# Attention probabilities turned by the DMA engines instead of TensorE, in a fused attention and gated feed-forward kernel

## The chip, the cores and the metric

The kernel runs on one core of a Trainium2 chip. Its metric is the device time of one execution in microseconds (us). The core has a matrix engine (TensorE, PE in the profile; its weight loads are listed apart as PEld), three engines for element-wise work (VectorE = DVE, ScalarE = ACT, GpSimd = POOL), a queue that here issues all transfers (SyncE = SP), and 16 DMA engines that carry them. Each engine works off its own list of instructions in order; an instruction that waits for a semaphore holds back everything behind it on its engine.

## The reference

The kernel computes attention with 4 batches, 8 heads, 768 positions and a head size of 64, and a gated feed-forward layer behind it, all in float32:

```python
scores = scale * np.matmul(q, k.transpose(0, 1, 3, 2))
keep = is_global | is_local            # 8 global columns, 96 local ones
scores = np.where(keep, scores + bias, -1e9)
a = np.exp(scores - np.max(scores, axis=-1, keepdims=True))
a = a / (np.sum(a, axis=-1, keepdims=True) + 1e-09)
attn = np.matmul(a, v)                 # then laid out as x: 3072 x 512
gate = 1.0 / (1.0 + np.exp(-(x @ w_gate)))
val = x @ w_val
return (gate * val @ w_out)            # d_ff = 1536
```

## The kernel before

The 3072 tokens are cut into 8 **blocks** of 384 tokens (index `bi`, `NB` = 384), two to a batch. A block's attention is done in 12 **items** `(s, t)`: `s` is one of 4 pairs of heads, `t` one of 3 tiles of 128 tokens. A block's feed-forward part is done in 12 **units** `f`, one for each slice of 128 of `d_ff`. Float32 products are made of three products of split operands (a high part and a low one, `xh`/`xl`, `w1h`/`w1l`, `w2h`/`w2l`, `hh`/`hl`).

A unit is `ff_in` (L527: twelve matmuls into the PSUM bank `ps_g`, twelve into `ps_u`, with a tanh on ScalarE at L545, a product on VectorE at L554, the split into `hh` on ScalarE at L557 and into `hl` on VectorE) and, later, `ff_out` (L561: nine matmuls into `ps_o`). The weights of `ff_out` are split again for each unit (L217 on ScalarE, then GpSimd). The weight conversion that the first part of the program needs is over when the third block's attention starts.

An item runs through these steps:

- `scores` (L359): matmuls into `ps_s`, then on VectorE two fused "add a table, take the minimum" instructions (L406), then on ScalarE two exponentials with their sums (L419). The query positions of a block's tile see a window of 256 key columns, 128 for the first tile of a batch.
- `normalise` (L425): on VectorE the sum's reciprocal (L434, L436) and two products (L438) in the tile `sb`, named `work` in the profile.
- `transposes` (L440): on TensorE four transposes of 128x128 (two for a batch's first tile) into the PSUM bank `ps_t` (L449), then one copy of that bank to `pT` in SBUF, on ScalarE (L457) for all blocks that this text is about.
- `values` (L460), after three items of each of two pairs of heads: matmuls with `pT` (L476) for the third block on into `ps_t` and `ps_v`, then `xh` on ScalarE (L518) and `xl` on VectorE (L519). The result is the `x` of the next block's feed-forward units.

From the third block on (`bi > PAIR`, `PAIR` = 1) a block's 12 items go beside the 12 units of the block before it, one item to a unit. `split_step` (L331) prepares `ks` and `qs` for a pair of heads on ScalarE, VectorE and GpSimd; `load_step` (L289) loads a pair's inputs through SP.

The order of the code sets priorities only: a scheduler at build time lays the instructions of each engine into a fixed order, and each engine keeps to it. Tiles that are named with `bufs` share so many buffers, and a writer waits until the last reader of its buffer is done. SP issues all loads and stores in one fixed order too.

Of the kernel before, what the change touches and what calls it, by code (L numbers as in the profile page):

```python
# [8 lines left out]
F32 = mybir.dt.float32  # L9
# [3 lines left out]
I16 = mybir.dt.int16  # L13
# [6 lines left out]
P = 128  # L20
# [8 lines left out]
def attn_moe_kernel(ctx, tc, qT, kT, v, n_global, n_local, wg, wv, wo, out, B, H, S, D):  # L29
    nc = tc.nc  # L30
# [5 lines left out]
    TB = 3  # L36
    NB = TB * P
    WORKB = 4
    OSTB = 4
    PTB = 3  # L40
    QB = 2
    SCALE = 1.0 / float(D) ** 0.5
# [13 lines left out]
    spool = inner.enter_context(tc.tile_pool(name="spool", bufs=2))  # L56
# [3 lines left out]
    late = {}  # L60
# [13 lines left out]
    words = cpool.tile([P, 2, 2], I32, name="words")  # L74
# [193 lines left out]
    PAIR = 1  # L268
    blocks = [(b, t0, TB) for b in range(B) for t0 in range(0, NTB, TB)]
# [14 lines left out]
    steps = {}  # L284
# [66 lines left out]
    def bank(*names):  # L351

        i = turns.get(names, 0)
        turns[names] = i + 1
        name = names[i % len(names)]
        pool = {"ps_s": ps_a, "ps_t": ps_a, "ps_v": ps_a, "ps_g": ps_gv, "ps_u": ps_gv}.get(name, ps_o)
        return pool.tile([P, 4 * P], F32, name=name)
# [82 lines left out]
    def transposes(bi, s, t):  # L440
        st = steps[bi, s]
        b, t0, nt = blocks[bi]
        n = 1 if t0 + t == 0 else 2
        sb, _ = st.pop(("s", t))
        pt = bank("ps_t", "ps_o0") if bi < PAIR else bank("ps_t")
        pt = pt.rearrange("p (c x) -> p c x", c=4)
        for j in range(2):
            for c in range(n):
                nc.tensor.transpose(pt[:, n * j + c], sb[:, j, c * P:(c + 1) * P], ident)  # L449
        if bi > PAIR and s % 2:  # L450
            pT = late["pool"].tile([P, 4, P], F32, name="pT2", bufs=PTB)
        else:
            pT = spool.tile([P, 4, P], F32, name="pT", tag="pT", bufs=PTB)
        if bi < PAIR and t > 0:
            nc.vector.tensor_copy(pT[:, 0:2 * n], pt[:, 0:2 * n])
        else:
            nc.scalar.copy(pT[:, 0:2 * n], pt[:, 0:2 * n])  # L457
        st["pT"][t] = pT

    def values(bi, pairs):  # L460
# [100 lines left out]
    def ff_out(bi, f):  # L561
# [26 lines left out]
        if f == NF - 1:  # L588
            for t in range(nt):
                ot = late["pool"].tile([P, DM], F32, name="ost", bufs=OSTB)  # L590
                if t == nt - 1 and end:
# [46 lines left out]
    def run(kind, bi, s, t):  # L638
        if kind == "S":
            if t == 0 and (bi, s) == (0, 0):  # L640
                ready_step((bi, s))
            scores(bi, s, t)
            if t == blocks[bi][2] - 1:
                i = all_steps.index((bi, s))
                if i + 1 < len(all_steps) and all_steps[i + 1] != (PAIR + 1, 0):
                    ready_step(all_steps[i + 1])
        elif kind == "T":
            normalise(bi, s, t)
            transposes(bi, s, t)
        else:  # L650
            if bi <= PAIR:
                values(bi, (s,))
            elif s % 2:
                values(bi, (s - 1, s))
# [153 lines left out]
    with tc.If(redo > 0):  # L808
        with tc.For_i(0, B, 1) as b:
            for t0 in range(0, NTB, TB):  # L810
                blocks.append((b, t0, TB))
                bi = len(blocks) - 1
# [45 lines left out]
```

## Time and profile before

| | |
|---|---|
| time, median of 3 runs | 772.47 us (769.70 to 772.59) |
| the profiled execution | 771.78 us, its span 770.0 us |
| TensorE clock granted, mean | 0.99 |
| TensorE busy | 755.6 us, 98% of the span |
| TensorE weight loads | 682.3 us, 89% |
| VectorE | 405.6 us, 53% |
| ScalarE | 408.8 us, 53% |
| GpSimd | 213.2 us, 28% |
| DMA moved | 57.01 MB, 74 GB/s over the span |

The span is the time from the first to the last instruction; some 2 us lie around it. A matmul's end is modelled, so what a group of matmuls costs is read from the distance of the starts, not from the busy time. Names such as `pT` or `work` are those of tiles; in `out<-in` the written tile stands first. A row of a timeline gives start and length in us; a row of a source line gives the shortest, the middle and the longest duration in ns.

### The profile page before, as it was taken

The numbers are of one execution on the slowest core, as the hardware profiler recorded it, in microseconds if no ns is written. First come the engines' busy times: TensorE is split into PE (matmuls) and PEld (weight loads), VectorE is DVE, ScalarE is ACT, GpSimd is POOL, SyncE is SP. The second block draws the span as 40 slices with busy tenths as digits, with TensorE's granted clock in tenths as the row PEclk, the third lists the DMA queues.
The fourth block names the chain that finished last, engine by engine and source line by source line (L and its number), as shares of the span: only waits on it lengthen the run. The fifth ranks groups of instructions, "written<-read, shape, count | busy, mean of one in ns | idle before, by whom it ended". The sixth has DMA issues, their size and how long they took to land. (4 is left out here: it accounts for less than half of the span.)

```text
span 770.0 us, 12641 instructions
## 1 busy us (share of the span) xinstructions
PE 755.6 (98%) x4661; PEld 682.3 (89%) x4661; DVE 405.6 (53%) x1085; ACT 408.8 (53%) x944; POOL 213.2 (28%) x164
## 2 busy tenths in 40 slices
PE   8999999999999999999999999999999999999996
PEld 5767678899999999999999999999999999999995
DVE  6789887556445555554565544454654565221111
ACT  4689876645546555553556554464555555432222
POOL 5424234332313323221232322222221222112222
PEclk7999999999999999999999999999999999999998
DMA  8768553403022121122113110221211200000001
GB/s 255 218 214 263 179 194 91 120 14 92 8 73 77 34 75 33 39 83 58 37 37 92 60 54 20 68 74 37 71 37 42 78 25 17 1 10 33 1 0 46
DMA packets 66982, 57.01 MB, mean 74 GB/s; under 512 B 17248, under 2 KB 59232, under 8 KB 66912
## 3 DMA queue, kind: packets, MB, share of 16 engines
q1 hardware_dynamic: 66912, 56.12, 24.7%
q8 instruction: 39, 0.64, 0.3%
q14 instruction: 31, 0.25, 0.1%
HBM read 49.81 MB, written 6.29 MB: 73 GB/s over the span
## 5 line engine op out<-in xcount | busy, mean ns | idle before, releaser
L180 POOL TENSOR_TENSOR w2l<-w2f,w2h 128x512 fp32r<-128x512 f32 x87 | 114.0, 1310 | 414.3 <-ACT w2h L217 406.3
L554 DVE SCALAR_TENSOR_TENSOR work<-work,ps_u 128x384 f32<-128x384 f32 x88 | 48.7, 553 | 216.7 <-PE ps_u L537 207.8
L537 PE MATMUL ps_u<-xh,w1l 128*128 128x384 f32 x384 | 134.4, 350 | 0.0
L537 PE MATMUL ps_g<-xh,w1l 128*128 128x384 f32 x384 | 131.3, 342 | 1.2 <-ACT work L545 1.2
L537 PE MATMUL ps_g<-xl,w1h 128*128 128x384 f32 x384 | 130.4, 339 | 0.7 <-DVE xl L519 0.7
L537 PE MATMUL ps_u<-xl,w1h 128*128 128x384 f32 x384 | 129.9, 338 | 0.0
L537 PE MATMUL ps_g<-xh,w1h 128*128 128x384 f32 x384 | 129.9, 338 | 0.0
L537 PE MATMUL ps_u<-xh,w1h 128*128 128x384 f32 x384 | 129.9, 338 | 0.0
L557 ACT ACTIVATE hh<-work 128x384 fp32r<-128x384 f32 x88 | 46.0, 522 | 128.0 <-DVE work L554 128.0
L419 ACT ACTIVATE work<-work,nms 128x256 f32<-128x256 f32 (+1 forms) x192 | 92.0, 481 | 27.4 <-DVE nms L406 27.0
L577 PE MATMUL ps_o<-w2l,hh 128*128 128x512 f32 x261 | 104.7, 401 | 0.7 <-POOL w2l L180 0.6
L577 PE MATMUL ps_o<-w2h,hh 128*128 128x512 f32 x261 | 102.7, 394 | 0.0
L577 PE MATMUL ps_o<-w2h,hl 128*128 128x512 f32 x261 | 102.6, 394 | 0.0
L217 ACT ACTIVATE w2h<-w2f 128x512 fp32r<-128x512 f32 x87 | 54.9, 631 | 89.6 <-PE ps_o L577 88.6
L180 DVE TENSOR_TENSOR hl<-work,hh 128x384 fp32r<-128x384 f32 x88 | 69.3, 788 | 28.9 <-ACT hh L557 28.7
L537 PEld LDWEIGHTS ps_g<-xh,w1l 128*128 128x128 f32 x384 | 72.3, 188 | 5.2 <-issue 2.6
L537 PEld LDWEIGHTS ps_g<-xl,w1h 128*128 128x128 f32 x384 | 72.2, 188 | 3.0 <-DVE xl L519 1.1
L537 PEld LDWEIGHTS ps_u<-xh,w1l 128*128 128x128 f32 x384 | 72.3, 188 | 1.1 <-issue 0.2
L537 PEld LDWEIGHTS ps_u<-xl,w1h 128*128 128x128 f32 x384 | 72.4, 189 | 0.5
L537 PEld LDWEIGHTS ps_g<-xh,w1h 128*128 128x128 f32 x384 | 72.2, 188 | 0.7
L537 PEld LDWEIGHTS ps_u<-xh,w1h 128*128 128x128 f32 x384 | 72.2, 188 | 0.2 <-issue 0.2
L406 DVE CUSTOM_DVE_ANT_0 work<-ps_s,tab 128x256 f32<-128x256 f32 x136 | 52.7, 420 | 25.4 <-PE ps_s L387 25.0
(131 smaller groups left out, 1169.1 us busy)
## 6 DMA issues: line engine op xcount, KB each, us to landing
qr<-in_qT SPq DMA_DIRECT2D x56, 192.0 KB, 3.3
kr<-in_kT SPq DMA_DIRECT2D x32, 192.0 KB, 2.6
v<-in_v SPq DMA_DIRECT2D x32, 192.0 KB, 3.1
raw<-in_w_gate SPq DMA_DIRECT2D x12, 512.0 KB, 4.2
raw<-in_w_val SPq DMA_DIRECT2D x12, 512.0 KB, 5.8
raw<-in_w_out SPq DMA_DIRECT2D x12, 512.0 KB, 3.8
out<-ost SPq DMA_DIRECT2D x24, 256.0 KB, 2.2
v<-in_v SPq DMA_DIRECT2D x16, 144.0 KB, 2.7
```

Source lines behind the costliest of these rows:

```text
L180: eng.tensor_tensor(out, a, b, op=ALU.subtract)
L217: ins = nc.scalar.activation(hi, w, AF.Copy)
L406: ins = nc.vector.tensor_tensor_reduce(sb[:, j, :w], ps[j][:, :w], (tabs0 if zero else tabs)[2 * s + j], -SCALE, 3.0e38, op0=ALU.add, op1= ...
L419: ins = nc.scalar.activation(sb[:, j, :w], sb[:, j, :w], AF.Exp, scale=-1.0, bias=nm[:, j:j + 1], accum_out=sm[:, j:j + 1])
L537: nc.tensor.matmul(ps[:, :n], wt[f][:, i, c], xt[:, c, :n], start=(k == 0), stop=(k == 3 * NC - 1))
L554: nc.vector.scalar_tensor_tensor(a[:, :n], a[:, :n], 1.0, pss[1][:, :n], op0=ALU.add, op1=ALU.mult)
L557: nc.scalar.activation(hh[:, :n], a[:, :n], AF.Copy)
L577: ins = nc.tensor.matmul(outs[bi][t], ht[:, t * P:(t + 1) * P], wt, start=(f == 0 and k == 0), stop=(f == NF - 1 and k == len(parts) - 1),)
```

## The change

For the blocks from the third on, `transposes` no longer uses TensorE. VectorE takes the 32-bit probabilities apart into two planes of 16-bit halves (two copies into `halves`, one for the low and one for the high halves of all columns); one DMA transpose on SP turns both planes from `halves` to `turned`; ScalarE copies the turned low halves and VectorE the turned high halves into the interleaved places of `pT`. `values` is unchanged. `halves` has one buffer, `turned` two, and the output tile `ost` has three buffers where it had four.

```diff
-    OSTB = 4
+    OSTB = 3
...
     def transposes(bi, s, t):
         sb, _ = st.pop(("s", t))
+        if bi > PAIR:
+            st["pT"][t] = transposes_by_dma(s, n, sb)
+            join(bi, s, t)
+            return
         pt = bank("ps_t", "ps_o0") if bi < PAIR else bank("ps_t")
...
+    def transposes_by_dma(s, n, sb):
+        m = 2 * n
+        halves = late["pool"].tile([P, 2 * 4 * P], I16, name="halves")[:, 0:2 * m * P]
+        words = sb[:, :, 0:n * P].bitcast(I16).rearrange("p j (x h) -> p j x h", h=2)
+        for h in range(2):
+            dst = halves[:, h * m * P:(h + 1) * m * P].rearrange("p (j x) -> p j x", j=2)
+            nc.vector.tensor_copy(dst, words[:, :, :, h])
+        turned = late["pool"].tile([P, 2 * 4, P], I16, name="turned", bufs=2)[:, 0:2 * m]
+        nc.sync.dma_start_transpose(turned, halves)
+        return turned
+
+    def join(bi, s, t):
+        turned = st["pT"][t]
+        m = 2 if blocks[bi][1] + t == 0 else 4
+        if s % 2:
+            pT = late["pool"].tile([P, 4, P], F32, name="pT2", bufs=PTB)
+        else:
+            pT = spool.tile([P, 4, P], F32, name="pT", tag="pT", bufs=PTB)
+        words = pT[:, 0:m].bitcast(I16).rearrange("p c (x h) -> p c x h", h=2)
+        nc.scalar.copy(words[:, :, :, 0], turned[:, 0:m])
+        nc.vector.tensor_copy(words[:, :, :, 1], turned[:, m:2 * m])
```

How the change moves instructions is shown at two places. The first is VectorE in the sixth block's attention, between two items of its second pair of heads. Before, the normalising products (L438) of an item are followed by the unit's product (L554) and at once by the next item's minima (L406):

```order
L438 TENSOR_SCALAR work<-work,rc 128x256 x2
L554 SCALAR_TENSOR_TENSOR work<-work,ps_u 128x384
L406 ISA work,nms<-ps_s,tab_123 128x256
L406 ISA nms 128x1
L406 ISA work,nms<-ps_s,tab_124 128x256
L406 ISA nms 128x1
L180 TENSOR_TENSOR ks<-kr,ks 64x576 x2
L180 TENSOR_TENSOR hl<-work,hh 128x384
L434 TENSOR_SCALAR sm<-sm 128x2
```

With the change the same stretch reads:

```order
L438 TENSOR_SCALAR work<-work,rc 128x256 x2
L468 COPY halves<-work 128x512 x2
L580 SCALAR_TENSOR_TENSOR work<-work,ps_u 128x384
L483 COPY pT_4953<-turned 128x512
L406 ISA work,nms<-ps_s,tab_123 128x256
L406 ISA nms 128x1
L406 ISA work,nms<-ps_s,tab_124 128x256
L406 ISA nms 128x1
L180 TENSOR_TENSOR ks<-kr,ks 64x576 x2
L180 TENSOR_TENSOR hl<-work,hh 128x384
L434 TENSOR_SCALAR sm<-sm 128x2
```

The copies into `halves` stand behind the products, and the copy out of `turned`, which waits for the item's DMA transpose, stands ahead of the next item's minima. So it is for four of the six items between two groups of `values`; for the other two the copy out of `turned` stands behind the next item's minima. The second place is ScalarE in the same stretch, with the change:

```order
L571 ACTIVATE work<-ps_g 128x384
L217 ACTIVATE w2h<-w2f_163 128x512
L482 COPY pT_4953<-turned 128x512
L343 ACTIVATE ks<-kr 64x576 x2
L345 ACTIVATE qs<-qr 128x2x384
L583 ACTIVATE hh<-work 128x384
L419 ACTIVATE work,sm<-work,nms 128x256 x2
L571 ACTIVATE work<-ps_g 128x384
```

Before, the copy from `ps_t` (L457) stood where the copy from `turned` (L482) stands now; the rows around it are in the same order. On TensorE the only rows that go are 264 transposes (L449); on SP 72 DMA transposes (L470) are set between the loads.

More of the change, by code (lines that the diff above doesn't have):

```diff
@@ L449, in transposes @@
                 nc.tensor.transpose(pt[:, n * j + c], sb[:, j, c * P:(c + 1) * P], ident)
[L450 to L453, printed above, removed]
+        pT = spool.tile([P, 4, P], F32, name="pT", tag="pT", bufs=PTB)
         if bi < PAIR and t > 0:
@@ L457, in transposes @@
             nc.scalar.copy(pT[:, 0:2 * n], pt[:, 0:2 * n])
+        st["pT"][t] = pT
+    def transposes_by_dma(s, n, sb):
[9 more added lines that the diff above has]
+    def join(bi, s, t):
+        st = steps[bi, s]
+        turned = st["pT"][t]
[3 more added lines that the diff above has]
+        else:
+            pT = spool.tile([P, 4, P], F32, name="pT", tag="pT", bufs=PTB)
+        words = pT[:, 0:m].bitcast(I16).rearrange("p c (x h) -> p c x h", h=2)
+        nc.scalar.copy(words[:, :, :, 0], turned[:, 0:m])
+        nc.vector.tensor_copy(words[:, :, :, 1], turned[:, m:2 * m])
         st["pT"][t] = pT
```

## The prediction

> **What bounds the kernel now.** I read the table of engines first, then busy time by stretches of the span in the stage that changes (from about 150 to 680 us).
>
> ```profile
> PE 755.6 (98%) x4661; PEld 682.3 (89%) x4661; DVE 405.6 (53%) x1085; ACT 408.8 (53%) x944; POOL 213.2 (28%) x164
> ```
> ```profile
> core 0: us, PE busy (x) PEld busy (x) DVE busy (x) ACT busy (x) POOL busy (x), PEclk, DMA share, GB/s
> 250.00:350.00 100.00, 100.00 (x635) 93.77 (x634) 54.94 (x150) 53.40 (x128) 27.77 (x18) 1.00 0.20 55
> 450.00:550.00 100.00, 100.00 (x643) 92.92 (x640) 49.42 (x141) 51.76 (x123) 24.23 (x17) 1.00 0.19 55
> ```
>
> TensorE has no gap there, and its clock is at full speed (1.00), so whatever leaves its list shortens the span, as long as the rest keeps up. VectorE and ScalarE stand idle almost half the time, the DMA engines four fifths. So the question is a balance: what TensorE sheds, against a longer path from score to `pT`.
>
> The pace of the stage is read from the groups of `values` (L476); there are 12, one for every six items. The first, two in a block without a batch's first tile, and the last:
>
> ```profile
> 181.90 1.31 PE L476 MATMUL ps_t<-pT,v 128*64 128x128 f32 x20
> ...
> 448.65 1.53 PE L476 MATMUL ps_t<-pT,v 128*64 128x128 f32 x24
> 494.51 1.53 PE L476 MATMUL ps_t<-pT,v 128*64 128x128 f32 x24
> ...
> 674.38 1.53 PE L476 MATMUL ps_t<-pT,v 128*64 128x128 f32 x24
> ```
>
> 674.38 - 181.90 = 492.5 us for 11 distances: 44.8 us for six items on average. With six wide items it is 45.9 (448.65 to 494.51); the other half of the groups, which hold two narrow items each (a batch's first tile), is then at about 43.7.
>
> **What TensorE sheds.** A transpose's modelled duration says little; I take the starts around four of them, and around two (a batch's first tile).
>
> ```profile
> 345.86 0.34 PE L537 MATMUL ps_g<-xh,w1h 128*128 128x384 f32 x1
> 346.04 0.60 PE L449 MATMUL ps_t<-ident,work 128*128 128x128 f32 x4
> 346.39 0.42 PE L537 MATMUL ps_u<-xh,w1l 128*128 128x384 f32 x1
> 346.65 0.34 PE L537 MATMUL ps_u<-xl,w1h 128*128 128x384 f32 x1
> 346.82 0.34 PE L537 MATMUL ps_u<-xh,w1h 128*128 128x384 f32 x1
> ...
> 363.59 0.38 PE L449 MATMUL ps_t<-ident,work 128*128 128x128 f32 x2
> 363.73 0.43 PE L537 MATMUL ps_u<-xl,w1h 128*128 128x384 f32 x1
> 363.99 0.34 PE L537 MATMUL ps_u<-xh,w1h 128*128 128x384 f32 x1
> ```
>
> Feed-forward matmuls start every 0.17 us (346.65 to 346.82). From 346.04 to 346.65 pass 0.61 us with one such matmul in it: 0.61 - 0.17 = 0.44 us for four transposes. Likewise 363.99 - 363.59 - 0.17 = 0.23 us for two. Of the 6 x 12 = 72 items 60 have four and 12 have two: 60 x 0.44 + 12 x 0.23 = 29.2 us, or 2.4 us per six items. TensorE's own pace becomes 44.8 - 2.4 = 42.4 us; 45.9 - 2.6 = 43.3 in wide groups, 43.7 - 2.2 = 41.5 in the others.
>
> **What is added, and where it waits.** ScalarE's copy from PSUM gives way to a copy of as many elements; I set it equal. VectorE gets three copies of 512 16-bit elements per item. Their nearest row is L203, 16-bit with a stride, which has 432 ns in the middle. That is 3 x 0.43 = 1.3 us on about 4 us of work per unit: VectorE doesn't fill up. But the copies stand in a row with the DMA transpose. In VectorE's order four of six items go: copies into `halves`, wait for the transfer, copy out of `turned`, and only then the next item's minima. So a loop forms, and its length per item is a sum of rows plus L, the time from the end of `halves` to `turned`:
>
> ```profile
> L203 DVE TENSOR_SCALAR neg<-raw x13: 407/432/1547, 14.4 to 124.1; 128x512 int16<-128x512 int16 x12, 128x1024 int16<-128x1024 int16 x1
> 342.17 0.41 DVE L406 CUSTOM_DVE_ANT_0 work<-ps_s,tab 128x256 f32<-128x256 f32 x1
> 342.96 1.27 DVE L180 TENSOR_TENSOR ks<-kr,ks 64x448 fp32r<-64x448 f32 x2
> 342.10 1.18 ACT L343 ACTIVATE ks<-kr 64x448 fp32r<-64x448 f32 x2 [2.03 <-PE ps_s L387]
> 343.30 0.85 ACT L345 ACTIVATE qs<-qr 128x768 fp32r<-128x768 f32 x1
> 344.06 0.51 ACT L557 ACTIVATE hh<-work 128x384 fp32r<-128x384 f32 x1
> 344.47 0.49 ACT L419 ACTIVATE work<-work,nms 128x256 f32<-128x256 f32 x1
> 345.45 0.61 ACT L217 ACTIVATE w2h<-w2f 128x512 fp32r<-128x512 f32 x1
> ...
> 347.72 0.17 DVE L436 RECIPROCAL rc<-sm 128x2 f32<-128x2 f32 x1
> 347.92 0.62 DVE L438 TENSOR_SCALAR work<-work,rc 128x256 f32<-128x256 f32 x2
> ```
>
> Copy out 0.43; from the first minimum's start to the end of both exponentials 0.41 + 0.1 for the hand-over + 0.98 (344.47 to 345.45) + 0.1 = 1.6; sum and reciprocal 2 x 0.2 (347.72 to 347.92); products 0.62; copies into `halves` 0.86; in all 3.9 us. GpSimd lengthens some of these:
>
> ```profile
> 346.14 1.51 POOL L180 TENSOR_TENSOR w2l<-w2f,w2h 128x512 fp32r<-128x512 f32 x1
> 346.42 1.26 DVE L434 TENSOR_SCALAR sm<-sm 128x2 f32<-128x2 f32 x1
> ...
> L434 DVE TENSOR_SCALAR sm<-sm x72: 153/169/1347, 139.1 to 662.7; 128x2 f32<-128x2 f32 x72
> L434 DVE TENSOR_SCALAR sm<-sm 128x2 f32<-128x2 f32 x72 | 24.4, 339 | 33.2 <-ACT work L419 33.2
> L457 ACT COPY pT<-ps_t 128x512 f32<-128x512 f32 x72 | 41.5, 576 | 6.6 <-PE ps_t L449 6.6
> L519 DVE TENSOR_TENSOR xl<-ps_t,xh 128x384 fp32r<-128x384 f32 x16 | 8.9, 554 | 4.7 <-ACT xh L518 4.5
> L406 DVE CUSTOM_DVE_ANT_0 work<-ps_s,tabs 128x128 f32<-128x128 f32 x26 | 6.6, 287 | 8.6 <-PE ps_s L387 8.6
> L419 ACT ACTIVATE work<-work,nms 128x128 f32<-128x128 f32 x32 | 12.5, 392 | 13.2 <-DVE nms L406 12.9
> ```
>
> An instruction on two numbers took 1.26 us and ended as GpSimd's did. The mean of L434 is 0.34 us against 0.17 in the middle; for this and the like on the products and copies I add 0.5 us. A close item then takes 4.4 us + L. In the other two items minima and exponentials run during the transfer: 4.4 - 1.6 = 2.8 us + L. Once in six items ScalarE puts copy, `ks`, `qs` and `hh` (the copy as L457, 0.58 + 1.18 + 0.85 + 0.51 = 3.1 us) ahead of the exponentials where VectorE needs 0.8: 2.3 more. Once, the two `xl` (2 x 0.55, L519) take 0.8 that nothing hides. Six items: 4 x 4.4 + 2 x 2.8 + 2.3 + 0.8 = 26.3 us + 6 L. Half the groups hold two narrow items, each shorter by about 1.1 us (a minimum 0.29 for 0.41 us, an exponential 0.39 for 0.49, twice each but overlapping: 0.4; products and four copies on half the columns, at the same rate: 0.7): on average **25.2 us + 6 L** against TensorE's 42.4.
>
> Stalled like this, VectorE and ScalarE are late with the tanh that frees `ps_g` (L571 with the change, behind the exponentials) and with the product that frees `ps_u`; there TensorE would wait.
>
> **L is not in the trace.** Nearest are the transfers that are there (KB each, median us from issue to landing):
>
> ```profile
> out<-ost SPq DMA_DIRECT2D x24, 256.0 KB, 2.2
> v<-in_v SPq DMA_DIRECT2D x32, 192.0 KB, 3.1
> raw<-in_w_val SPq DMA_DIRECT2D x12, 512.0 KB, 5.8
> ```
> ```profile
> 344.23 1.85 POOL L180 TENSOR_TENSOR qs<-qr,qs 128x768 fp32r<-128x768 f32 x1 [4.93 <-ACT qs L345]
> 344.26 0.39 SPq L309 DMA_DIRECT2D kr<-in_kT  x1
> 344.70 0.48 SPq L310 DMA_DIRECT2D kr<-in_kT  x1
> ```
>
> Lower end: `out` moves the same 256 KB from SBUF in 2.2 us. Upper end: the slowest row, 5.8 us. In between `v`, in short runs of 512 bytes, takes 3.1; a transpose handles runs of 256 bytes. SP started 0.03 us after VectorE's `ks` ended (342.96 + 1.27 = 344.23). I take L = 2.9 us, between `out` and `v` and nearer to `v`.
>
> The Trainium skill (DMA: Bandwidth & Descriptors, Latency and other measured facts) gives DMA transposes an effective 261 GB/s; for 256 KB that is an estimated 1.0 us of moving, which would put L near the lower rows. No run here shows it yet.
>
> **The sum.** With L = 2.9, wide groups need 26.3 + 17.4 = 43.7 us, TensorE there 43.3: 0.4 x 6 groups = 2.4 us of stalls. Groups with two narrow items need 43.7 - 2.2 = 41.5, as much as TensorE: none. On SP some transposes stand behind five loads of 0.4 to 0.5 us issue each, which the loads' own waits mostly let pass in time; I add 0.5 us in each of the same 6 groups, 3 us. One output buffer less costs nothing: the stores land in 2.2 us, and the next three come a block later. So 771.8 - 29.2 + 2.4 + 3.0 = 748.0 us for the profiled execution; the median lies 0.7 above it: **749 us**. TensorE-bound with no stall it would be 743; L = 2.2 gives that too (25.2 + 13.2 = 38.4).
>
> **Rivals.**
> - *The loop decides* (slower). The place is the copy out of `turned` ahead of the minima; the point is 25.2 + 6 L = 44.8, so L = 3.27 us. At L = 3.9 six items take 48.6, 3.8 more than before, 12 times: 772.5 + 46 = 818. For it: the point lies only 0.4 us above my L, and each 0.1 us on a copy counts three times per item. Against it: `out` at 2.2, and DMA engines busy a fifth of the time.
> - *The two cancel* (same): L at 3.2 to 3.3, 769 to 776 us.
> - *The transfer goes piece by piece.* An item has eight 128x128 pieces; if each costs an issue of 0.48 us (the row of L310) ahead of a landing of 2.2, L is 6.0, and 25.2 + 36 = 61.2, 16.4 more, 12 times: 969 us. Against it: there is one instruction on SP for all eight. The upper end of L (5.8) gives 60.0 and 955.
>
> The Trainium skill (VectorE: DVE Perf Modes, The three transpose paths) lists 390 ns for a 128x128 16-bit transpose on TensorE and 1309 ns by DMA, and advises TensorE where PSUM will do; eight in turn would be an estimated 10.5 us, six of which would make about 88 us per six items and some 1290 us in all. The trace's own price on TensorE is 0.11 us per float32 transpose in the stream, so that table holds latencies, and its 1309 may too.
>
> **Chances.** Forecast 0.59; the loop decides 0.24; the two cancel 0.10; piece by piece 0.07. The likeliest case alone spans 742 (no stall) to 767. The range for 8 in 10 goes to 830: the loop at L = 4.1. Beyond it lie piece by piece and the loop's far end, some 0.15 together, and below 741 some 0.03. Faster by over 0.5% (what can be told from no change): 0.59; same 0.10; slower 0.31.
>
> **What would show it.** Right: distances between groups of `values` of 42.5 to 43.5 us, a DMA transpose landing in under 3 us, waits of `ps_g` and `ps_u` small. Wrong: TensorE idle before L563 on ScalarE's tanh or VectorE's L580, and VectorE idle before L483 on the DMA; landing over 3.3 us; copies of 0.6 us or more. If L is short and TensorE still waits, the loop is mis-summed.

## The result, and the profile after

The changed kernel takes **800.93 us** (median of 4 runs, 797.83 to 803.18) against 771.09 us for the kernel before in the same series: a ratio of 1.038, 95% interval 1.035 to 1.041. It is slower by 30 us where 22 less were forecast. The forecast was wrong in sign, and what came is the rival that was called "the loop decides".

The table of engines and two stretches of the stage, changed kernel, read as those before:

```profile
PE 739.5 (93%) x4397; PEld 660.9 (83%) x4397; DVE 507.9 (64%) x1301; ACT 409.4 (51%) x944; POOL 212.5 (27%) x164
```
```profile
250.00:350.00 100.00, 90.21 (x545) 83.19 (x544) 67.47 (x174) 49.39 (x120) 23.11 (x16) 0.98 0.33 79
450.00:550.00 100.00, 94.27 (x555) 87.56 (x554) 65.64 (x176) 51.16 (x121) 24.01 (x17) 0.95 0.34 80
```

TensorE has 264 instructions fewer and is no longer full: 90 and 94 us of 100, at 545 and 555 matmuls where there were 635 and 643. No other engine is near full either. The granted clock is 0.98 and 0.95 in these stretches; before it was 1.00.

The pace comes from the groups of `values` (L502 in this kernel), which one row sums up, first and last start of a matmul:

```profile
L502 PE MATMUL ps_t<-pT,v x264: 272/273/324, 181.8 to 701.7; 128*64 128x128 f32 x132
```

The last matmul starts 1.2 us behind its group's start (before: 675.6 and 674.38). So 701.7 - 1.2 - 181.8 = 518.7 us for 11 distances, **47.15 us for six items** where before it was 44.8. The 2.4 us more, 11 times, are the 26 us by which the span grew (770.0 to 796.1).

The waits of the changed kernel (in all, times, longest, in us), and the landings of the transfer:

```profile
ACT pT L482 <- DMA turned<-halves: 158.6, 66, 6.8
ACT hh L583 <- DVE work L580: 127.5, 56, 3.7
DVE pT L483 <- DMA turned<-halves: 127.5, 62, 4.5
PEld ps_g L563 <- ACT work L571: 26.6, 14, 4.5
PE ps_g L563 <- ACT work L571: 23.0, 14, 4.1
PE ps_u L563 <- DVE work L580: 4.3, 3, 1.6
```
```profile
L470 SPq DMA_TRANSPOSE turned<-halves x72: 1197/1248/2165, 139.6 to 696.5; - x72
DMA to landing us min/median/max: 2.4/3.1/4.8
```

VectorE waits for the transfer in 62 of 72 items and ScalarE in 66. VectorE's wait was one sign given for the rival, and TensorE's wait before L563 on ScalarE's tanh (L571) another. Here is how they hang together, in VectorE's and then ScalarE's timeline around 500 us:

```profile
489.02 0.76 DVE L468 COPY halves<-work 128x512 int16<-128x512 int16 x2
492.94 0.46 DVE L483 COPY pT<-turned 128x512 int16<-128x512 int16 x1 [3.16 <-DMA turned<-halves]
493.30 0.54 DVE L580 SCALAR_TENSOR_TENSOR work<-work,ps_u 128x384 f32<-128x384 f32 x1
493.75 0.42 DVE L406 CUSTOM_DVE_ANT_0 work<-ps_s,tab 128x256 f32<-128x256 f32 x1
...
496.46 1.79 DVE L468 COPY halves<-work 128x512 int16<-128x512 int16 x2
498.18 0.54 DVE L580 SCALAR_TENSOR_TENSOR work<-work,ps_u 128x384 f32<-128x384 f32 x1
501.42 0.46 DVE L483 COPY pT<-turned 128x512 int16<-128x512 int16 x1 [2.69 <-DMA turned<-halves]
...
504.55 1.85 DVE L180 TENSOR_TENSOR hl<-work,hh 128x384 fp32r<-128x384 f32 x1 [0.61 <-ACT hh L583]
...
506.71 1.46 DVE L438 TENSOR_SCALAR work<-work,rc 128x256 f32<-128x256 f32 x2
508.20 0.76 DVE L468 COPY halves<-work 128x512 int16<-128x512 int16 x2
```
```profile
501.42 0.79 ACT L482 COPY pT<-turned 128x512 int16<-128x512 int16 x1 [5.14 <-DMA turned<-halves]
502.07 1.17 ACT L343 ACTIVATE ks<-kr 64x448 fp32r<-64x448 f32 x2
...
505.40 0.47 ACT L571 ACTIVATE work<-ps_g 128x384 f32<-128x384 f32 x1
```

The end of `halves` at 489.02 + 0.76 = 489.78, the copy out at 492.94: L = 3.16 us, and 3.17 in the next item (498.25 to 501.42). In both the copy out stands ahead of the next item's minima. In the second, ScalarE waited 5.14 us for the transfer, then made `ks`, `qs`, `hh` and the exponentials, and only then the tanh at 505.40, for which TensorE waited 2.35 us (its L563 starts at 505.93). From one end of `halves` to the next pass 8.47 us (489.78 to 498.25) and 10.71 us (498.25 to 508.96); a sixth of TensorE's 42.4 would be 7.1.

A loop that is set by L has the form c + 6 L for six items. From this run c = 47.15 - 6 x 3.15 = **28.2 us** as a mean over the 11 distances, where the prediction had 25.2. These two numbers, 28.2 and 3.15, are what the experiments test.

### The profile page after: what moved, and what is told of

Same layout as the page of the kernel before. It is cut to its first block, busy times and chain, and to the rows that moved or that the text cites. A ratio compares the mean times of both kernels' runs of the same rounds, so it can differ in the third digit from the quotient of the medians.

```text
span 796.1 us, 12415 instructions
## 1 busy us (share of the span) xinstructions
PE 739.5 (93%) x4397; PEld 660.9 (83%) x4397; DVE 507.9 (64%) x1301; ACT 409.4 (51%) x944; POOL 212.5 (27%) x164
## 3 DMA queue, kind: packets, MB, share of 16 engines
q1 hardware_dynamic: 136800, 73.43, 36.4%
## 5 line engine op out<-in xcount | busy, mean ns | idle before, releaser
L180 POOL TENSOR_TENSOR w2l<-w2f,w2h 128x512 fp32r<-128x512 f32 x87 | 116.0, 1334 | 393.2 <-ACT w2h L217 393.1
L563 PE MATMUL ps_g<-xh,w1l 128*128 128x384 f32 x384 | 135.0, 352 | 23.0 <-ACT work L571 23.0
L563 PE MATMUL ps_u<-xh,w1l 128*128 128x384 f32 x384 | 130.4, 340 | 4.5 <-DVE work L580 4.3
L482 ACT COPY pT<-turned 128x512 int16<-128x512 int16 (+1 forms) x72 | 52.4, 728 | 158.7 <-DMA turned<-halves 158.6
L563 PE MATMUL ps_g<-xl,w1h 128*128 128x384 f32 x384 | 131.9, 344 | 2.1 <-DVE xl L545 2.1
L563 PE MATMUL ps_g<-xh,w1h 128*128 128x384 f32 x384 | 132.1, 344 | 0.0
L563 PE MATMUL ps_u<-xh,w1h 128*128 128x384 f32 x384 | 129.9, 338 | 0.0
L563 PE MATMUL ps_u<-xl,w1h 128*128 128x384 f32 x384 | 129.8, 338 | 0.0
L483 DVE COPY pT<-turned 128x512 int16<-128x512 int16 (+1 forms) x72 | 36.4, 506 | 127.7 <-DMA turned<-halves 127.5
L563 PEld LDWEIGHTS ps_g<-xh,w1l 128*128 128x128 f32 x384 | 73.8, 192 | 30.7 <-ACT work L571 26.6
L180 DVE TENSOR_TENSOR hl<-work,hh 128x384 fp32r<-128x384 f32 x88 | 65.8, 748 | 25.3 <-ACT hh L583 24.9
L563 PEld LDWEIGHTS ps_u<-xh,w1l 128*128 128x128 f32 x384 | 72.2, 188 | 9.0 <-DVE work L580 6.6
L563 PEld LDWEIGHTS ps_g<-xl,w1h 128*128 128x128 f32 x384 | 74.0, 193 | 3.6 <-DVE xl L545 2.7
L563 PEld LDWEIGHTS ps_g<-xh,w1h 128*128 128x128 f32 x384 | 73.9, 192 | 0.0
L563 PEld LDWEIGHTS ps_u<-xl,w1h 128*128 128x128 f32 x384 | 72.2, 188 | 2.0
L180 POOL TENSOR_TENSOR qs<-qr,qs 128x768 fp32r<-128x768 f32 x24 | 44.7, 1861 | 109.0 <-ACT qs L345 101.4
```

The lines of the kernel that those rows point to most:

```text
L180: eng.tensor_tensor(out, a, b, op=ALU.subtract)
L482: nc.scalar.copy(words[:, :, :, 0], turned[:, 0:m])
L483: nc.vector.tensor_copy(words[:, :, :, 1], turned[:, m:2 * m])
L563: nc.tensor.matmul(ps[:, :n], wt[f][:, i, c], xt[:, c, :n], start=(k == 0), stop=(k == 3 * NC - 1))
```

## The experiments

Three theories stood against each other: *the loop* (the copies out of `turned` wait in the engines' lists ahead of work that the next item needs), *the added work* (VectorE's three copies per item, or the traffic, cost the time wherever they stand), and *a part of the loop* (the wait counts in some items only). Times are medians over three rounds for both copies set late, and single executions else; each is set against the kernel before on the same chip (769 to 772 us).

### All the work, but `pT` does not wait for it

TensorE and ScalarE do what they did before the change. VectorE's copies into `halves`, the DMA transposes and a copy out of `turned` run beside them.

```diff
         if bi > PAIR:
-            st["pT"][t] = transposes_by_dma(s, n, sb)
-            join(bi, s, t)
-            return
+            turned = transposes_by_dma(s, n, sb)
+            m = 2 * n
+            back = late["pool"].tile([P, 4, P], I16, name="back")
+            pending.append((back[:, 0:m], turned[:, m:2 * m]))   # copied on VectorE behind the next minima
...
```

> TensorE turns the probabilities as in the kernel before and ScalarE copies them from PSUM; beside that VectorE makes the two copies into halves, SP issues the DMA transposes, and VectorE copies one turned plane to a tile that nobody reads, behind the next item's minima. It has all of the change's work on VectorE and all of its traffic, without the path through the DMA. The loop: 771 to 776 us, as before, since VectorE has room. Work or traffic decides: 795 us or more.

Measured: 769.52 us, against 769.15 before. The groups of `values` (ps_t, L515 here) and the table of engines:

```profile
PE 753.4 (98%) x4661; PEld 681.3 (89%) x4661; DVE 485.6 (63%) x1301; ACT 407.4 (53%) x944; POOL 213.8 (28%) x164
```
```profile
L515 PE MATMUL ps_t<-pT,v x264: 272/273/324, 179.6 to 673.3; 128*64 128x128 f32 x132
```

VectorE works 80 us more than before (485.6 against 405.6) and the traffic is there, and the pace is 44.8 us (673.3 - 1.2 - 179.6 = 492.5 over 11), as before. VectorE waits for a transfer ahead of the copy out 12 times, and nothing else needs that copy. The added work alone costs nothing; that theory falls.

### The changed order without the wait

The copies out read a weight tile that doesn't change. To keep the scheduler from laying out another program, here and in the next experiments with "same order" the instructions of each engine are chained in the order they have in the changed kernel (an order edge from each to the next, no wait; only the DMA transposes are left out of the chain). In the traces of these four runs the instructions of TensorE, VectorE, ScalarE and GpSimd stand in the changed kernel's order, one for one. `turned`, which nobody reads here, has one buffer.

```diff
     def join(bi, s, t):
-        turned = st["pT"][t]
+        turned = w1l[0].bitcast(I16).rearrange("p i c x -> p (i c) x")[:, 0:8, 0:P]
...
```

> The copies out read a weight tile that never changes instead of the transposed halves (so the output is wrong); the DMA transposes still run and nobody waits for them, and the order on every engine is that of the changed kernel. The loop: 742 to 750 us, VectorE's and ScalarE's waits for the DMA gone, TensorE at 42.4 to 42.7 us per six items. Added work, or the traffic: 795 to 805 us. If the free order alone made the earlier kernel without a wait slow (767 us), this one must be well below that.

Measured: 743.36 us. TensorE's groups, same columns as above:

```profile
L502 PE MATMUL ps_t<-pT,v x264: 272/273/324, 178.7 to 647.4; 128*64 128x128 f32 x132
```

That is 42.5 us for six items (467.5 over 11); the prediction's pace of TensorE without the transposes was 42.4. Same instructions, same places, 57.6 us less: the whole loss is the wait for the transfer and what is queued behind it.

### A shorter and a longer transfer, in the same order

In the first only one of an item's eight pieces is transposed, and the copies out read that piece for all eight; in the second every transfer is issued twice.

```diff
-        nc.sync.dma_start_transpose(turned, halves)
+        nc.sync.dma_start_transpose(turned[:, 0:1], halves[:, m * P:(m + 1) * P])   # short
...
```
```diff
         nc.sync.dma_start_transpose(turned, halves)
+        nc.sync.dma_start_transpose(turned, halves)                                 # twice
```

> One of an item's eight pieces is transposed instead of all, and the copies out read that piece for all (so the output is wrong), and every instruction of TensorE, VectorE, ScalarE and GpSimd and every load is held to the order of the changed kernel. The time from halves to turned should fall from 3.16 us by the 0.9 us that the landings differ by, to 2.26. If the loop in this order decides (six items take the greater of TensorE's 42.4 us and 28.2 + 6 L, the 28.2 calibrated on the changed kernel's 47.15 us at L = 3.16): 28.2 + 13.6 = 41.8, TensorE decides, 801 - 12 x 4.75 = 744 us, with uneven groups up to 755. If the wait counts only in half of the items: 801 - 12 x 2.7 = 769. If the added work or collisions decide: no change, 795 to 805.

> Every DMA transpose is issued twice, the same halves to the same place, and the copies out wait for both; the order on TensorE, VectorE, ScalarE and GpSimd and of the loads is that of the changed kernel. SP holds each transpose for about 1.25 us, so the second lands 1.2 to 1.5 us later and L becomes 4.4 to 4.6 us. The loop: 28.2 + 6 x 4.4 to 4.6 = 54.6 to 55.8 us per six items, 7.5 to 8.7 more than the changed kernel, 12 times: 890 to 905 us. If the wait counts only in half of the items: 845 to 855. Work: 795 to 810.

Measured: 753.3 us and 1024.68 us. Short (groups of `values`, then two of VectorE's rows), and twice (VectorE, then SP):

```profile
L503 PE MATMUL ps_t<-pT,v x264: 272/273/324, 176.9 to 657.5; 128*64 128x128 f32 x132
```
```profile
458.69 0.76 DVE L468 COPY halves<-work 128x512 int16<-128x512 int16 x2
461.80 0.47 DVE L484 COPY pT<-turned 128x512 int16<-128x512 int16 x1 [2.34 <-DMA turned<-halves]
```
```profile
L503 PE MATMUL ps_t<-pT,v x264: 272/273/475, 200.4 to 928.6; 128*64 128x128 f32 x132
```
```profile
504.53 1.79 DVE L468 COPY halves<-work 128x512 int16<-128x512 int16 x2
512.59 0.45 DVE L484 COPY pT<-turned 128x512 int16<-128x512 int16 x1 [6.27 <-DMA turned<-halves]
```
```profile
506.39 1.23 SPq L470 DMA_TRANSPOSE turned<-halves  x1
509.49 1.23 SPq L471 DMA_TRANSPOSE turned<-halves  x1
```

The second transfer started 3.10 us behind the first: since it writes the same place, the program lets it wait on a semaphore until the first has landed. I had overlooked that and taken 1.25. So L was 6.27 us, not 4.5, and the expected time missed by 120 us. With the L that was there the loop's formula holds: 28.2 + 6 x 6.27 = 65.8 us, measured 66.1 (728.2 - 1.2 = 727.0 over 11). From L = 3.15 to 6.27 the slope is (66.1 - 47.15) / 3.12 = **6.1** per six items; all six waits count, and the theory of a part falls for transfers of this length. The short one, with L = 2.35, gives 28.2 + 14.1 = 42.3, a tie with TensorE; measured 43.6, 1.1 above TensorE's own pace. Here VectorE waits for the transfer in 57 items only (in 70 with two transfers): in the item with `ks` its own work mostly lasts longer than the short transfer, and that item doesn't get shorter with it. With five of six items shortened by 0.8 us the sum would be 47.15 - 4.0 = 43.15; what is left to 43.6 isn't explained.

### What the constant lacked: GpSimd

In the same order, GpSimd computes only 64 of the 512 columns of each `w2l`, and TensorE reads these for all.

> GpSimd computes only 64 of the 512 columns of each w2l, and TensorE reads these 64 for all (so the output is wrong); TensorE's, VectorE's and ScalarE's work, the DMA transposes and the order on every engine are those of the changed kernel. In the changed kernel's six items from 469 to 517 us, VectorE's instructions beside GpSimd's take 6.3 us longer than their undisturbed length, where the prediction allowed 3.0; w2l is there in six of some eight cases. If that is what the sum lacked: 28.2 - 4 to 5 = 23.2 to 24.2 us, + 6 x 3.16 = 42.2 to 43.2 per six items against TensorE's 42.4, 745 to 765 us. If the sum lacked something else (ScalarE's longer copies, the order): 790 to 801.

```diff
-        issue_after(split(hi, lo, w2f[f].bitcast(F32)), last_gate[-1])
+        w = w2f[f].bitcast(F32)
+        issue_after(nc.scalar.activation(hi, w, AF.Copy), last_gate[-1])
+        sub(nc.gpsimd, lo[:, 0:64], w[:, 0:64], hi[:, 0:64])
...
+            wl = wl[:, 0:64].rearrange("p (a x) -> p a x", a=1).to_broadcast([P, 8, 64])
```

Measured: 765.04 us, 36 less than the changed kernel, and 44.4 us for six items (489.5 - 1.2 = 488.3 over 11). Its groups of `values`, and two groups of VectorE's:

```profile
L504 PE MATMUL ps_t<-pT,v x264: 272/273/324, 179.4 to 668.9; 128*64 128x128 f32 x132
```
```profile
L470 DVE COPY halves<-work 128x512 int16<-128x512 int16 (+1 forms) x144 | 52.5, 407 | 2.3
L436 DVE TENSOR_SCALAR sm<-sm 128x2 f32<-128x2 f32 x72 | 12.0, 166 | 27.2 <-ACT work L421 27.2
```

The same two groups of VectorE (mean ns behind the busy time), and GpSimd's `w2l` beside one of them, in the changed kernel:

```profile
L468 DVE COPY halves<-work 128x512 int16<-128x512 int16 (+1 forms) x144 | 69.2, 523 | 2.3
L434 DVE TENSOR_SCALAR sm<-sm 128x2 f32<-128x2 f32 x72 | 19.4, 269 | 27.2 <-ACT work L419 27.2
```
```profile
496.35 1.29 POOL L180 TENSOR_TENSOR w2l<-w2f,w2h 128x512 fp32r<-128x512 f32 x1 [5.42 <-ACT w2h L217]
```

The pair of copies at 496.46 took 1.79 us where 0.76 is usual: it ended 0.6 us behind the end of GpSimd's instruction (497.64). In the cycle from 468.5 to 516.5 us such lengthenings beside `w2l` and `qs` add up to 6.3 us (1.31, 0.73, 1.04, 1.29, 0.85 and 1.04), against the 3.0 that the prediction allowed. The run gives 2.75 us per six items back.

This edit also shortens TensorE's own wait for `w2l`, 8.2 us in all in the changed kernel (0.7 per six items), but the gain is not from there. VectorE's timelines, added up from the start of each copy out to the end of the next copies into `halves`, the 13th to the 66th item, give 28.42 us per six items in the changed kernel, 24.67 of it busy and 3.75 idle, and 25.37 in this run, 21.49 busy and 3.88 idle. A wait for TensorE would be idle time; what got shorter is VectorE's instructions. In the short run and the one with two transfers the same sum is 28.5 and 28.1 us: the constant is there at every L.

The Trainium skill (SBUF — State Buffer, SBUF: two separate sides) says that VectorE, in a two-port mode or with two inputs from SBUF, and GpSimd share a port pair as an exclusive lock: whichever starts first holds it for a whole instruction, and the other is fully blocked. The row at 496.46 fits that: the pair ended 0.6 us behind GpSimd's instruction, most of its own 0.76 us, as if it had waited for GpSimd's end. No run here shows in which mode these copies are.

### The copies out set late

Both copies are put behind the next item's minima and exponentials (order edges, with no change in what is computed).

```diff
-            join(bi, s, t)
+            pending.append((bi, s, t))
...
+    def join_pending(behind):
+        while pending:
+            a, d = join(*pending.pop(0))          # ScalarE's copy, VectorE's copy
+            if behind:
+                issue_after(a, last_exp[-1])
+                issue_after(d, last_min[-1])
```

It is called with True behind an item's `scores` and with False ahead of `values`.

> The copies out of turned are put behind the next item's minima on VectorE and behind its exponentials on ScalarE, for all items but the last before a group of values. Same work, same transfers, outputs unchanged. Theory 'loop' (engines that work in order stand still for L = 3.16 us ahead of the next item's minima; with the changed kernel's 47.15 us per six items the loop is 28.2 us + 6 L): three to four of the six items lose 1.6 us each from the loop, so 47.15 - 4.8 to 6.4 = 40.8 to 42.3 us, below TensorE's 42.4: 743 to 752 us. Theory 'work' (the three more copies on VectorE and their collisions with GpSimd cost the time, wherever they stand): 795 to 805 us as before. Theory 'ScalarE' (ScalarE's copy ahead of the tanh is what holds TensorE): the tanh still stands behind the copy, 780 us or more.

Measured, three rounds: **739.92 us** (739.2 to 741.8) against 771.51; ratio 0.959, interval 0.957 to 0.962. It beats both kernels, and it is 3 us below the range expected of the loop. Table of engines, waits, groups:

```profile
PE 724.2 (98%) x4397; PEld 656.1 (89%) x4397; DVE 492.4 (67%) x1301; ACT 411.7 (56%) x944; POOL 216.5 (29%) x164
```
```profile
DVE pT L492 <- DMA turned<-halves: 17.8, 13, 2.8
```
```profile
L512 PE MATMUL ps_t<-pT,v x264: 272/273/324, 176.8 to 645.7; 128*64 128x128 f32 x132
```

The same work and the same landings (3.1 us in the middle) at 42.5 us for six items. In VectorE's list 58 of the 72 copies out now stand behind the following item's copies into `halves`: a copy out starts 9.4 us in the middle behind the end of its own copies into `halves`, where it was 3.16, and VectorE waits 13 times instead of 62.

Two more runs set only one of the copies late, and a third the `values` one unit later as well:

> Only VectorE's copy out of turned is set behind the next item's minima; ScalarE's copy stays where the changed kernel has it, in most items ahead of the next exponentials. If a waiting copy holds up what is queued behind it: the minima now run during the transfer and the exponentials still wait, so each of the four close items saves VectorE's copy and one minimum, 0.9 us: 28.2 - 3.7 + 19.0 = 43.5 us per six items, 750 to 765 us. If the blocked ScalarE alone (tanh behind the copy) holds TensorE: 790 to 801.

> Only ScalarE's copy out of turned is set behind the next item's exponentials; VectorE's copy stays ahead of the next minima as in the changed kernel. The exponentials still come after minima that wait, so the close items keep their length, and only the one with ks, qs and hh on ScalarE gets shorter, by 2.3 us: 25.9 + 19.0 = 44.9 us per six items, 768 to 780 us. If VectorE's place alone makes the loop: 790 to 801. If ScalarE's alone does: 740 to 755.

> Both copies out set late as in the fast version (739.9 us), and the values one unit later, so that the third item's copies too can stand behind the next item's minima. TensorE was 98% busy in the fast version, at its own pace of 42.5 us per six items: 737 to 742 us, no gain beyond what can be measured.

Measured: 777.58 us with VectorE's copy late, 767.08 with ScalarE's, 742.27 with `values` late too. In pace, from the first and last starts of the groups as above (179.4 to 681.6, 181.4 to 671.0, 183.9 to 650.1), that is 45.5, 44.4 and 41.8 us (in the third the last group is stretched over 6.3 us, where it is 1.2 else). So neither copy alone makes the loop: of the 4.65 us per six items between the changed kernel (47.15) and 42.5, ScalarE's copy left in its place keeps 3.0, VectorE's 1.9. These shares are rough, since the scheduler was free apart from the new edges: with ScalarE's copy late it also put VectorE's ahead of the next minima in only 34 of 72 items, where it was 41. The first of these runs gave less than expected (45.5 instead of 43.5). Its timeline shows why; these three rows are waits of VectorE on ScalarE or on the one buffer of `halves`:

```profile
476.20 0.76 DVE L468 COPY halves<-work 128x512 int16<-128x512 int16 x2 [1.76 <-DMA turned<-halves]
...
481.30 0.56 DVE L180 TENSOR_TENSOR hl<-work,hh 128x384 fp32r<-128x384 f32 x1 [1.84 <-ACT hh L592]
...
489.52 1.27 DVE L180 TENSOR_TENSOR ks<-kr,ks 64x448 fp32r<-64x448 f32 x2 [2.86 <-ACT ks L343]
```

`hh` and `ks` stand behind ScalarE's copy, which still waits for the transfer, and VectorE's minima of the next item then meet `hl` or `ks` anyway. The wait went round by the other engine. With `values` a unit later nothing is gained in time (742.27 us): TensorE is full already.

### Three runs that the scheduler changed

The first runs had left the order free. The same edit for a short transfer, two transfers per item (one for each plane), and copies that read a tile of zeros:

```diff
-        nc.sync.dma_start_transpose(turned, halves)
+        for h in range(2):
+            nc.sync.dma_start_transpose(turned[:, h * m:(h + 1) * m], halves[:, h * m * P:(h + 1) * m * P])
```
```diff
-        turned = st["pT"][t]
+        turned = late["still"]        # 128x1024 zeros
```

> Only one of an item's eight 128x128 pieces is transposed, and both copies out read this piece again and again, with as many elements as before: attention values are not computed, the work on all engines is as much. L falls by what the other seven pieces take. 'Loop': at a landing of 2.3 us (as small loads have) L is 2.35 and the loop 28.2 + 14.1 = 42.3, as much as TensorE: 743 to 752 us; at 2.7 it is 28.2 + 16.5 = 44.7: 771 us. 'Work': 795 to 805 us.

> Each item's transpose is split into two on SP, one for each plane; outputs unchanged, all else alike. The second starts only when SP is free again, 1.25 us after the first by the changed kernel's trace, and moves half, so L of the high plane grows by 0.6 to 1.2 us. 'Loop': 6 x 0.6 to 1.2 = 3.6 to 7.2 us more per six items, 12 times: 844 to 887 us. 'Work': VectorE, ScalarE and GpSimd do the same, 797 to 805 us.

> The copies out read a tile that was filled once with zeros, so that nothing waits for a DMA transpose; the copies into halves and all 72 transposes are still done, but attention values are not computed. The scheduler moves the copies forward since nothing holds them. 'Loop': no L in it, TensorE's 42.4 us per six items decide: 743 to 750 us. 'Work': the copies and their collisions are all there, 790 us or more; also so if the transfers disturb others by their traffic.

Measured: 796.51, 789.13 and 766.96 us, all far from what was expected of the loop. By the first two numbers alone I would have dropped L as the cause. But VectorE's list had changed with the edit. With the short transfer the place shown ahead of the prediction reads (order of VectorE):

```
L438 TENSOR_SCALAR work<-work,rc 128x256 x2
L468 COPY halves<-work 128x512 x2
L484 COPY pT<-turned 128x512
L581 SCALAR_TENSOR_TENSOR work<-work,ps_u 128x384
L406 ISA work,nms<-ps_s,tab_123 128x256
```

The copy out stands directly behind `halves`, ahead of the unit's product: 24 of 72 copies stand so, where it was 13. The scheduler places it by the time that it gives the transfer; a transfer that it takes for shorter is waited for sooner. In free order the short transfer saves some 4 us at most (796.51, where the changed kernel's runs go from 797.83 to 803.18), in the same order some 48 (800.93 to 753.3). With two transfers the landings were 2.4 us each in the middle, so that the first plane came 0.7 us sooner than the whole had; that run is 12 us faster than the changed kernel, and since its order moved too, no more is read from it.

In the run without a wait, `pT` is ready early, and the scheduler cut `values` into 85 pieces between other matmuls where the run in the same order has 20. Without a wait and in free order, then without a wait and in the same order, TensorE's groups of `values`:

```profile
L505 PE MATMUL ps_v<-pT,v 128*64 128x128 f32 x344 | 33.6, 284 | 0.4 <-DVE pT L456 0.4
L505 PE MATMUL ps_t<-pT,v 128*64 128x128 f32 x360 | 32.5, 284 | 0.0
```
```profile
L502 PE MATMUL ps_t<-pT,v 128*64 128x128 f32 x360 | 23.2, 277 | 0.0
L502 PE MATMUL ps_v<-pT,v 128*64 128x128 f32 x344 | 22.8, 283 | 0.5 <-DVE pT L456 0.5
```

The same matmuls keep TensorE busy for 66.1 us in pieces and 46.0 together, a difference of 20 us where the two runs differ by 24 (the first is the slower one).

## Why the prediction was wrong, point by point

- **What bounds the kernel, and what TensorE sheds: right.** 29.2 us were to leave TensorE's list and its pace to become 42.4 us for six items. Two runs in which TensorE is hardly kept waiting show 42.5, and 743.36 and 741.80 us in the profiled executions against 743 us for "TensorE-bound with no stall". One reading under it was off: it set 45.9 us for wide groups and 43.7 for the others. The distances before are 39.4 us for the first and 43.6 to 46.8 for the other ten; with both copies late they are 36.4 and 42.7 to 43.4. A short first distance pulls the mean down, and narrow items don't set the groups apart as the prediction's 43.3 and 41.5 do.
- **Work on VectorE: right.** 1.3 us per item was to find room; it costs nothing where `pT` doesn't wait for it (769.52 against 769.15 us). The copies were 0.42 us (`halves`) and 0.46 us (`pT`) in the middle, 0.43 in the sum.
- **ScalarE's copy "set equal" to L457's 0.576 us: wrong, without effect.** It took 0.78 us. In the one place where it entered (copy, `ks`, `qs`, `hh` = 3.1 us), the rows give 3.0 from 501.42 to the exponentials at 504.42, since the next instruction starts 0.65 us behind the copy's start.
- **The form of the loop: right.** c + 6 L, with a slope of 6.1 measured.
- **L = 2.9 us: too small by 0.25.** 3.15 us measured from `halves` to the copy, like the landing of `v` (3.1) and not of `out` (2.2). That is 6 x 0.25 = 1.5 us per six items. The Trainium skill's 261 GB/s (DMA: Bandwidth & Descriptors, Latency and other measured facts), which it gives for a non-contiguous middle dimension, is close to it: seven further pieces, 224 KB, moved the landing from 2.2 to 3.1 us, some 250 GB/s. At that rate an estimated 0.1 of the first piece's 2.2 us are moving. The Trainium skill's 1309 ns for a 128x128 transpose by DMA (VectorE: DVE Perf Modes, The three transpose paths) is not the price of each of eight in one transfer: the seven further ones cost 0.13 us each.
- **The constant, 25.2 us: too small by 3.0. This is the step that failed.** Its items in the cycle from 468.5 to 516.5 us, where "close" is an item with the copy out ahead of the next minima and "loose" one with it behind them: with the two `xl` 5.0 beside L (5.2 predicted); loose with `ks` 4.7 (2.8); loose 2.2 (2.8); close 5.3 (4.4); close with `ks`, `qs`, `hh` 7.5 (6.7); the narrow one 4.4 (3.3); 29.1 in all. Each that exceeds its price holds an instruction beside GpSimd. "For this and the like I add 0.5 us" was an average over all of an engine's instructions in a kernel in which nothing waited for them; in the loop the lengthenings are 6.3 us per six items, 1.05 per item. With GpSimd's `w2l` cut to an eighth the constant falls to 44.4 - 18.9 = 25.5. The number of close items erred the other way: it is 41 of 72, 3.4 of six where the sum had four.
- **The rival's point, L = 3.27: off by the same step.** With c = 28.2 it lies at (44.8 - 28.2) / 6 = 2.8 us. So even my own L would have made the kernel slower: 28.2 + 17.4 = 45.6 against 44.8. What I called a matter of L, 0.4 us from its point, was decided by the constant: with the predicted one even L = 3.15 would have left 25.2 + 18.9 = 44.1, below 44.8.
- **Sum of the misses.** Forecast 42.6 (loop), measured 47.15: 1.5 from L and 3.0 from the constant. 12 x (47.15 - 42.4) = 57 us of stalls on TensorE, where 5.4 were forecast: 771.8 - 29.2 + 57 = 800. The gain of 29 us was there and was given back twice over.
- **"Piece by piece": ruled out**, by a landing of 3.1 us and one issue of 1.25 us on SP. The 3 us set down for SP weren't tested apart.
- **The range** (741 to 830) held the time; the forecast had been given 0.59, the loop 0.24. The rival came, but not by its condition: L stayed under its point of 3.27. "If L is short and TensorE still waits, the loop is mis-summed" is the sentence that applied.

## What to carry to other kernels

A transfer of 3 us that replaces work on a full engine is worth only as much as the list of the engine that waits for it allows: look for what stands directly behind the waiting copy, and put the copy one item later before judging the transfer (the same work took 801 us and 740 us). When two sides of a balance differ by a few per cent, price each instruction of the chain in the company it will have, beside GpSimd above all, and not by the mean over the kernel. And an experiment on a scheduled program says little while the scheduler may answer it: hold the order, then change one thing.

## What the runs showed of the hardware

- A DMA transpose within SBUF lands 2.2 us after its issue for one 128x128 piece of 16 bits and 3.1 us for eight; SP is held 1.1 and 1.25 us.
- A 16-bit copy of 128x512 with a stride on one side takes 0.42 to 0.46 us on VectorE and 0.78 us on ScalarE.
- TensorE's granted clock was below 1.00 in stretches in which TensorE stalled (0.98 and 0.95 here, 0.91 on average in the run with 1024.68 us), and 1.00 in the same stretches of the runs without. What of a stall's price is this was not separated.
